# Loading and normalising x around the weight loads in a recurrent memory transformer block

## The chip, the cores and the metric

The kernel runs on one core of a Trainium2 chip. The core has a matrix engine (PE, with its own weight loads, PEld), a vector engine (DVE), a scalar engine (ACT), a general engine (POOL) and a queue engine (SP), and 16 DMA engines which all queues share. A DMA is issued from the queue of SP, ACT or POOL. The metric is the time of one execution on the device, in microseconds (us). The kernel before took 3471.91 us, the median of five runs from 3450.73 to 3481.48.

## The reference, cut to what matters

The reference computes a forward pass and all its gradients, in bf16. x has 2048 rows of 448 columns. Layer norm comes first, then an attention that walks over x in 64 segments of 32 rows and carries 8 memory rows from one segment to the next, then a gated feed-forward layer:

```python
for s in range(n_seg):                                   # 64 segments of 32 rows
    h = concatenate([mem, x[:, s*32:(s+1)*32]], axis=1)  # 8 memory rows and 32 of layernorm(x)
    q, k, v = h @ Wq, h @ Wk, h @ Wv                     # 448 -> 16 heads of 256
    p = softmax(where(mask, q @ k.T * scale, -1e9))
    o = (p @ v) @ Wo                                     # 16 * 256 -> 448
    mem = o[:, :8]                                       # goes into the next segment
    outs.append(o[:, 8:])
h  = x + attention(layernorm(x))
h2 = h + (silu(n @ w_gate) * (n @ w_up)) @ w_down        # n = layernorm(h)
```

The outputs are h2 and the gradients of x, mem0, the four attention weights and the three weights of the feed-forward layer. Segment s + 1 cannot start before segment s has given its memory rows, so the 64 segments are one chain, forwards and, for the gradients, backwards.

## The kernel before

The program has four phases: `forward_chain` (to about 1200 us of the trace), `ffn_phase`, `backward_chain` and `tail_phase`. Only the first is touched by the change. Everything lives in a few big arenas: `W` holds Wq, Wk, Wv and Wo (448 rows in `KC` = 4 chunks of 128, the last chunk half full and padded with zeros), `A` and `B` hold working tiles, and `A(kb, ...)` is a view that begins at that kilobyte. Two views at the same kilobytes are the same memory, and the framework makes the later user wait for the earlier.

How one segment runs (lines 375 to 476). The input of a segment stands in `hT_roll`, transposed: for each of the 4 chunks, 12 windows of 40 columns, 32 for rows of x and 8 for memory rows. `wpass` (line 353) multiplies Wq and then Wk with the segment's window: 128 matmuls each at line 360, cast out of PSUM by `k.evac` (line 75 on DVE, line 77 on ACT). Then come the scores (391), V (399), the softmax (403 to 416, with Exp on ACT at 409), the turned probabilities (420), the heads' outputs (428), and the output projection with Wo for the memory rows alone (437). The 8 memory rows are summed by a small matmul (446) and copied by DVE into the next window (449). Each segment stores qT, kT, the probabilities and V for the backward pass (451 to 454), and every fourth runs the projection for the 128 rows (462). `qT_b`, `kT_b` and `V_b` have two buffers each, used in turn. The heads' outputs of four segments stand in `xblk_b[t % 2]`, where t is the number of the group of 128 rows.

How x gets into the windows. `stats(t)` (line 311) loads tile t of x (128 rows) from SP or ACT in turn, into one of four places in `xblk_b[0]`; takes mean and variance on DVE (`ln_stats`, lines 82 and 84), the square root on ACT (86) and its reciprocal on DVE (87); writes the normalised tile into `xblk_b[1]` (319); and stores it to `XN` in DRAM (321). `prep_tile(t)` (line 338) reads it back with a DMA transpose on SP (342), and POOL copies it into four windows, one copy per chunk (345). The tile t + 2 is prepared in the first segment of group t (line 457), tiles 0 and 1 ahead of the loop.

What sets the order. The framework plans the order of every engine's instructions over the whole program, by priority and by its own estimate of when each can start, and then the order is fixed; an engine works through its list and stops at the first instruction that waits. What stands under `k.prio.crit()` has priority over the rest: in the kernel before, that is the chain of each segment. `tc.issue_after(ins)` makes the instructions under it stand behind `ins` in their engine's order. The weights are loaded from POOL, each as two DMAs (232, 233) followed by a memset of the padding (234), and Wo as one (328).

Of the kernel before, what the change touches and what calls it, by code (L numbers as in the profile page):

```python
# [229 lines left out]
def pad_rows(k, dst, src2d, eng):  # L230

    eng.dma_start(out=dst[:, 0:3, :], in_=src2d[0:3 * P, :].rearrange("(kc p) n -> p kc n", p=P))
    eng.dma_start(out=dst[0:64, 3, :], in_=src2d[3 * P:k.D, :])
    k.nc.gpsimd.memset(dst[64:P, 3, :], 0.0)
# [30 lines left out]
def forward_chain(k: _K):  # L265
    nc, tc = k.nc, k.tc
    S, D, M, H, Dh, HD = k.S, k.D, k.M, k.H, k.Dh, k.HD
    SEG, L, NSEG, NT, KC, DP, MC, DC = k.SEG, k.L, k.NSEG, k.NT, k.KC, k.DP, k.MC, k.DC
    X2 = k.aps["A_x"][0]
    MEM0 = k.aps["A_mem0"][0]  # L270
    ident, dr, sel, maskb = k.ident, k.dr, k.sel, k.maskb
    smal = k._small
# [8 lines left out]
    kT_b = [A(8 + 4 * i, 32, 64) for i in range(2)]  # L281
    V_b = [A(16 + 4 * i, 2048) for i in range(2)]
    stg_b = [A(24 + 4 * i, 2048) for i in range(2)]
    xblk_b = [A(32 + 8 * i, 32, P) for i in range(2)]
    mblk = A(48, 32, P)
    hT_flat = A(56, KC, NWIN * L + 24)
    hT_roll = hT_flat[:, :, 0:NWIN * L].rearrange("p k (w l) -> p k w l", l=L)
# [20 lines left out]
    nc.sync.dma_start(out=m0[0:M, 0:D], in_=MEM0)  # L308
    nc.vector.memset(m0[0:M, D:DP], 0.0)

    def stats(t):
        q = nc.sync if t % 2 == 0 else nc.scalar
        x_t = xblk_b[0].rearrange("p a b -> p (a b)")[:, (t % 4) * DP:(t % 4) * DP + D]
        q.dma_start(out=x_t, in_=X2[t * P:(t + 1) * P, :])
        mv = k.ln_stats(x_t, k.rstd1[:, t:t + 1], smal)
        xn = xblk_b[1].rearrange("p a b -> p (a b)")[:, (t % 4) * DP:(t % 4 + 1) * DP]
        if t < 4:
            nc.gpsimd.memset(xn[:, D:DP], 0.0)
        nc.vector.tensor_scalar(out=xn[:, 0:D], in0=x_t, scalar1=mv[:, 0:1], scalar2=k.rstd1[:, t:t + 1],
                                op0=ALU.subtract, op1=ALU.mult)  # L320
        q.dma_start(out=dr["XN"][t * P:(t + 1) * P, :], in_=xn)

    for t in range(2):
        stats(t)
    pad_rows(k, Wq_sb, k.Wq2, nc.gpsimd)
    pad_rows(k, Wk_sb, k.Wk2, nc.gpsimd)
    pad_rows(k, Wv_sb, k.Wv2, nc.gpsimd)
    nc.gpsimd.dma_start(out=Wo_sb, in_=k.Wo2.rearrange("(c p) d -> p c d", p=P))
    pm = k.ps1()
    pmh = pm[:].bitcast(BF16)  # L330
    for kc in range(KC):
        nc.tensor.transpose(pmh[:, kc * M:(kc + 1) * M], m0[0:M, kc * P:(kc + 1) * P], ident[0:M, 0:M])
    pm3 = pmh[:, 0:KC * M].rearrange("p (c m) -> p c m", m=M)
    nc.vector.tensor_copy(out=hT_roll[:, :, 0, SEG:L], in_=pm3)
    for t in range(2, NT):
        stats(t)

    def prep_tile(t):
        if t >= NT:
# [30 lines left out]
                                        in_=blk[:, 16 * hf:16 * hf + 16, :].rearrange("p c n -> p (c n)"))  # L370
            nc.gpsimd.dma_start(out=dr["X_o"][t][:, hf * 2048:(hf + 1) * 2048], in_=ot)

    prep_tile(0)
    prep_tile(1)
    for s in range(NSEG):
        t, r = divmod(s, 4)
        jm = s % 16
# [5 lines left out]
        with k.prio.crit():  # L383
# [57 lines left out]
            if s + 1 < NSEG:  # L441
                nc.vector.tensor_copy(out=om[:, 0:224], in_=pO[:, 0:224])
                nc.scalar.copy(out=om[:, 224:D], in_=pO[:, 224:D])
                pm = k.ps1()
                for kc in range(KC):
                    nc.tensor.matmul(pm[:, kc * M:(kc + 1) * M], lhsT=om[:, kc * P:(kc + 1) * P], rhs=sel[:, 0:M],  # L446
                                     start=True, stop=True)
                pm3 = pm[:, 0:KC * M].rearrange("p (c m) -> p c m", m=M)
                nc.vector.tensor_copy(out=hT_roll[:, :, (s + 1) % NWIN, SEG:L], in_=pm3)

        nc.gpsimd.dma_start(out=dr["QT"][s], in_=qT.rearrange("p c n -> p (c n)"))
        nc.sync.dma_start(out=dr["KT"][s], in_=kT.rearrange("p c n -> p (c n)"))
# [589 lines left out]
```

## Time and profile before

| what | value |
|---|---|
| median of five runs | 3471.91 us (3450.73 to 3481.48) |
| the profiled execution | 3470.52 us, its span 3468.7 us |
| granted PE clock, mean | 0.958 of full speed |
| PE busy, share of the span | 88% |
| DVE, ACT, POOL | 38%, 28%, 18% |
| first matmul of segment 0 | 39.19 us from the start |
| first matmul of segment 1 | 80.97 us |

Idle time of an engine is put down to what ended it: in `[35.80 <-POOL arA L345]` the engine was idle for 35.80 us, and what let it go was POOL's instruction of line 345 that wrote a tile of arena A. `SPq`, `ACTq` and `POOLq` are the queues that issue DMAs. The chain of work is followed back from the last instruction of the program, at each step to what released it, so what stands on it set the time. "issue" on it is time in which nothing that the profile shows was waited for. In the tables by stretch of time the columns are: the stretch, its length, busy time and number of instructions of PE, PEld, DVE, ACT and POOL, the granted PE clock, the busy share of the DMA engines, and GB/s.

### The profile page before, as it was taken

The numbers are of one execution on the slowest core, as the hardware profiler recorded it, in microseconds if no ns is written. First come the engines' busy times: TensorE is split into PE (matmuls) and PEld (weight loads), VectorE is DVE, ScalarE is ACT, GpSimd is POOL, SyncE is SP. The second block draws the span as 40 slices with busy tenths as digits, with TensorE's granted clock in tenths as the row PEclk, the third lists the DMA queues.
The fourth block names the chain that finished last, engine by engine and source line by source line (L and its number), as shares of the span: only waits on it lengthen the run. The fifth ranks groups of instructions, "written<-read, shape, count | busy, mean of one in ns | idle before, by whom it ended". The sixth has DMA issues, their size and how long they took to land.

```text
span 3468.7 us, 120965 instructions
## 1 busy us (share of the span) xinstructions
PE 3051.2 (88%) x55038; PEld 2061.0 (59%) x55038; DVE 1321.2 (38%) x2921; ACT 973.7 (28%) x2181; POOL 618.3 (18%) x1304
## 2 busy tenths in 40 slices
PE   3999999999999568992999998999999898998999
PEld 2677777777777445662666666666666454443444
DVE  4344444444444256771444444444444201111111
ACT  1333333333333222330333333333333102111100
POOL 3111111111111111111122122212211111111121
PEclk8999999999999879996999999999999899999999
DMA  7444633543444788899778777877877969788661
GB/s 263 131 130 130 177 127 130 161 145 129 153 134 142 162 187 178 195 219 232 147 155 176 156 172 164 174 155 169 169 166 154 301 195 195 166 177 171 160 247 38
DMA packets 997173, 583.91 MB, mean 168 GB/s; under 512 B 906100, under 2 KB 916420, under 8 KB 995060
## 3 DMA queue, kind: packets, MB, share of 16 engines
q1 hardware_dynamic: 926788, 340.27, 47.0%
q0 software_dynamic: 67568, 233.95, 19.9%
q8 instruction: 430, 7.05, 0.9%
q10 hardware_dynamic: 2304, 1.97, 0.2%
q14 instruction: 83, 0.68, 0.1%
HBM read 104.05 MB, written 250.19 MB: 102 GB/s over the span
## 4 chain that ended last, share of the span: by engine, by line
PE 61%; issue 13%; DMA 10%; DVE 8%; SPq 3%; ACT 2%; POOL 1%; ACTq 0%; DVEq 0%; POOLq 0%
PE psf L360 12%; PE po L756 8%; PE psf L399 6%; PE psf L713 5%; PE psf L691 4%; PE po L437 3%; PE fx L462 3%; PE fx L815 3%; PE psf L536 2%; PE psf L921 2%; PE psf L778 2%; PE psf L942 2%; PE psf L446 2%; DVE arA L75 2%; DVE arB L75 1%
## 5 line engine op out<-in xcount | busy, mean ns | idle before, releaser
L77 ACT CAST arA<-psf 128x320 bf16<-128x320 f32 (+4 forms) x1139 | 487.3, 447 | 1607.5 <-PE psf L360 423.5
L75 DVE CAST arA<-psf 128x384 bf16<-128x384 f32 (+6 forms) x1029 | 492.4, 496 | 1083.0 <-PE psf L921 363.7
L360 PE MATMUL psf<-arA,arW 128*128 128x40 bf16 x16384 | 433.4, 181 | 62.6 <-POOL arA L345 35.8
L360 PEld LDWEIGHTS <-arW 128*128 128x128 bf16 x16384 | 431.4, 97 | 77.5 <-issue 58.1
L756 PE MATMUL po<-arW,arA 128*32 128x448 bf16 x6144 | 359.7, 365 | 41.3 <-DVE arA L75 22.1
L921 PE MATMUL psf<-arW,arA 128*128 128x512 bf16 x990 | 254.1, 385 | 10.2 <-DMA arW<-X_k 4.6
L713 PE MATMUL psf<-arA,arW 128*128 128x40 bf16 x8192 | 218.7, 180 | 49.5 <-POOL arA L648 39.7
L399 PE MATMUL psf<-arW,arA 128*64 128x512 bf16 x2048 | 259.7, 382 | 0.0
L713 PEld LDWEIGHTS <-arW 128*128 128x128 bf16 x8192 | 214.4, 96 | 69.2 <-issue 68.7
L756 PEld LDWEIGHTS <-arA 128*32 128x32 bf16 x6144 | 156.0, 98 | 161.4 <-issue 32.7
L921 PEld LDWEIGHTS <-arA 128*128 128x128 bf16 x1440 | 136.1, 99 | 186.7 <-issue 42.5
L536 PE MATMUL psf<-arA,arW 128*128 128x256 bf16 x1344 | 164.1, 284 | 88.3 <-DMA arA<-arA 60.1
L536 PEld LDWEIGHTS <-arW 128*128 128x128 bf16 x1344 | 136.6, 102 | 118.1 <-issue 94.7
L399 PEld LDWEIGHTS <-arA 128*64 128x64 bf16 x2048 | 148.7, 111 | 65.2 <-issue 0.2
L75 DVE CAST arB<-psf 40x320 bf16<-40x320 f32 x320 | 107.8, 337 | 98.0 <-PE psf L428 64.5
L691 PEld LDWEIGHTS <-arW 128*128 128x128 bf16 x2048 | 88.6, 101 | 66.4 <-issue 62.8
L77 ACT CAST arB<-psf 128x96 bf16<-128x96 f32 (+1 forms) x320 | 98.2, 307 | 103.4 <-DVE arB L75 51.1
L723 ACT COPY arA<-psf 128x1024 bf16<-128x1024 bf16 x128 | 123.3, 1015 | 4.6 <-PE psf L722 3.0
L462 PE MATMUL fx<-arW,arA 128*128 128x448 bf16 x512 | 124.5, 353 | 0.0
L691 PE MATMUL psf<-arB,arW 128*128 128x80 bf16 x2048 | 99.5, 204 | 16.7 <-DVE arB L740 7.8
L437 PE MATMUL po<-arW,arB 128*8 128x448 bf16 x2048 | 109.4, 356 | 4.2 <-DVE arB L75 0.4
L942 PE MATMUL psf<-arW 128*128 128x448 bf16 x450 | 95.2, 361 | 5.7 <-DMA arW<-X_o 5.6
(232 smaller groups left out, 3769.0 us busy)
## 6 DMA issues: line engine op xcount, KB each, us to landing
QT<-arA POOLq DMA_DIRECT2D x64, 512.0 KB, 4.2
KT<-arA SPq DMA_DIRECT2D x64, 512.0 KB, 3.4
VG<-arA SPq DMA_DIRECT2D x64, 512.0 KB, 3.1
X_o<-arA POOLq DMA_DIRECT2D x40, 512.0 KB, 4.5
X_v<-arA POOLq DMA_DIRECT2D x32, 512.0 KB, 6.4
X_k<-arA POOLq DMA_DIRECT2D x32, 512.0 KB, 4.1
X_q<-arA POOLq DMA_DIRECT2D x32, 512.0 KB, 4.2
arW<-X_o SPq DMA_DIRECT2D x30, 512.0 KB, 14.2
```

What stands on the lines that cost most here:

```text
L75: nc.vector.tensor_copy(out=out, in_=in_)
L77: nc.scalar.copy(out=out, in_=in_)
L360: nc.tensor.matmul(pss[b][:, jj * L:(jj + 1) * L], lhsT=W_sb[:, kc, c * P:(c + 1) * P], rhs=hT_roll[:, kc, sl, :], start=(kc == 0), stop=( ...
L399: nc.tensor.matmul(pV[b][64 * g:64 * g + 64, 0:512], lhsT=hT_flat[:, kc, sl * L:sl * L + 64], rhs=Wv_sb[:, kc, n * 512:(n + 1) * 512], sta ...
L437: nc.tensor.matmul(pO[32 * (j % 4):32 * (j % 4) + M, 0:D], lhsT=o8[:, j, :], rhs=Wo_sb[:, cj(j), :], start=(j < 4), stop=(j >= MC - 4), sk ...
L462: nc.tensor.matmul(px[:, 0:D], lhsT=xblk[:, j, :], rhs=Wo_sb[:, cj(j), :], start=(j == 0), stop=(j == MC - 1))
L536: nc.tensor.matmul(ps[:, f2 * 256:(f2 + 1) * 256], lhsT=Wt[:, kc, c * P:(c + 1) * P], rhs=xT[:, kc, :], start=(kc == 0), stop=(kc == KC - 1))
L691: nc.tensor.matmul(ps[b][:, i * 2 * L:(i + 1) * 2 * L], lhsT=lhs[:, cl, :], rhs=rhs_bd[:, cl // 2, :, :].rearrange("p g n -> p (g n)"), st ...
L713: nc.tensor.matmul(pss[b][:, jj * L:(jj + 1) * L], lhsT=WoT_sb[:, kc, c * P:(c + 1) * P], rhs=do_roll[:, kc, sl, :], start=(kc == 0), stop ...
L756: nc.tensor.matmul(pH[32 * (j % 4):32 * (j % 4) + 32, 0:D], lhsT=blk[nm][:, j, r * SEG:(r + 1) * SEG], rhs=WT[:, cj(j), :], start=(nm == " ...
L921: nc.tensor.matmul(pa[2 * kc + g][:, 0:w], lhsT=lhs_of(b)[:, kc * P:(kc + 1) * P], rhs=rhs_of(b, g), start=(b == 0), stop=(b == nblk - 1), ...
L942: nc.tensor.matmul(pa[i][:, 0:D], lhsT=lhs_of(b, i), rhs=rhs_of(b), start=(bi == 0), stop=(bi == len(nblk) - 1))
```

## The change

The whole of x gets a place of its own, `xn_all`, 16 KB at `A(24)`, where it is loaded, normalised in place, and stored from. It lies over `stg_b` (first used in segment 3) and over `xblk_b[1]`, and the two halves of `xblk_b` are swapped, so that `xblk_b[1]` (now at `A(32)`) is first written in segment 4.

Tiles 0 and 1 are loaded by one DMA from SP, ahead of the weights. The weights are issued on POOL as before, but without the memsets in between; behind them, on the same queue, one DMA loads tiles 2 to 15; the three memsets come after that. The padding columns of all tiles are cleared by one memset on DVE.

The statistics of tiles 0 and 1 are taken under `k.prio.crit()`, with one square root for both, and the normalised tiles are turned by PE and copied into the windows by DVE and ACT (`by_pe`); they are still stored to XN, by one DMA for both. The statistics of tiles 2 to 15 are written behind segment 0's chain, and their `bn_stats` must stand behind the copy of line 449 (`to_h`) on DVE. They share one square root and one reciprocal, and are stored to XN by one DMA. Tile 2 is prepared in segment 2 instead of segment 0; the other tiles as before.

```diff
-    xblk_b = [A(32 + 8 * i, 32, P) for i in range(2)]
+    xblk_b = [A(40 - 8 * i, 32, P) for i in range(2)]
...
-    def stats(t):
-        q = nc.sync if t % 2 == 0 else nc.scalar
-        x_t = xblk_b[0].rearrange("p a b -> p (a b)")[:, (t % 4) * DP:(t % 4) * DP + D]
-        q.dma_start(out=x_t, in_=X2[t * P:(t + 1) * P, :])
-        mv = k.ln_stats(x_t, k.rstd1[:, t:t + 1], smal)
-        xn = xblk_b[1].rearrange("p a b -> p (a b)")[:, (t % 4) * DP:(t % 4 + 1) * DP]
...
-        q.dma_start(out=dr["XN"][t * P:(t + 1) * P, :], in_=xn)
-
-    for t in range(2):
-        stats(t)
-    pad_rows(k, Wq_sb, k.Wq2, nc.gpsimd)
-    pad_rows(k, Wk_sb, k.Wk2, nc.gpsimd)
-    pad_rows(k, Wv_sb, k.Wv2, nc.gpsimd)
+    xn_all = A(24, NT, DP)
+    x_rows = X2.rearrange("(t p) d -> p t d", p=P)
+    xn_rows = dr["XN"][0:S, :].rearrange("(t p) d -> p t d", p=P)
+    nc.sync.dma_start(out=xn_all[:, 0:2, 0:D], in_=x_rows[:, 0:2])
+    for Wd_sb, Ws in ((Wq_sb, k.Wq2), (Wk_sb, k.Wk2), (Wv_sb, k.Wv2)):
+        nc.gpsimd.dma_start(out=Wd_sb[:, 0:3, :], in_=Ws[0:3 * P, :].rearrange("(kc p) n -> p kc n", p=P))
+        nc.gpsimd.dma_start(out=Wd_sb[0:64, 3, :], in_=Ws[3 * P:D, :])
     nc.gpsimd.dma_start(out=Wo_sb, in_=k.Wo2.rearrange("(c p) d -> p c d", p=P))
...
-    for t in range(2, NT):
-        stats(t)
+    nc.gpsimd.dma_start(out=xn_all[:, 2:NT, 0:D], in_=x_rows[:, 2:NT])
+    nc.vector.memset(xn_all[:, :, D:DP], 0.0)
+    for Wd_sb in (Wq_sb, Wk_sb, Wv_sb):
+        nc.gpsimd.memset(Wd_sb[64:P, 3, :], 0.0)
+    mv_all = smal.tile([P, NT, nc.vector.BN_AGGR_DIM], FP32, name="mv_all", bufs=1)
+    sd_all = smal.tile([P, NT], FP32, name="sd_all", bufs=1)
+
+    def by_pe(t):
+        pt = k.ps1()[:].bitcast(BF16)
+        for kc in range(KC):
+            nc.tensor.transpose(pt[:, kc * P:(kc + 1) * P], xn_all[:, t, kc * P:(kc + 1) * P], ident[:, :])
+        for kc in range(KC):
+            k.evac(hT_roll[:, kc, 4 * t:4 * t + 4, 0:SEG], pt[:, kc * P:(kc + 1) * P].rearrange("p (g j) -> p g j", g=4),
+                   "vs"[kc % 2])
+
+    def stats(t0, t1, ins):
+
+        def placed(fn):
+            if ins is None:
+                return fn()
+            with tc.issue_after(ins):
+                return fn()
+        for t in range(t0, t1):
+            st6 = smal.tile([P, nc.vector.BN_STATS_DIM], FP32, name="stats")
+            placed(lambda: nc.vector.bn_stats(out=st6[:], in_=xn_all[:, t, 0:D]))
+            nc.vector.bn_aggr(out=mv_all[:, t, :], in_=st6[:])
+        nc.scalar.activation(out=sd_all[:, t0:t1], in_=mv_all[:, t0:t1, 1], func=ACT.Sqrt, bias=k.eps_t[:], scale=1.0)
+        nc.vector.reciprocal(out=k.rstd1[:, t0:t1], in_=sd_all[:, t0:t1])
+        for t in range(t0, t1):
+            nc.vector.tensor_scalar(out=xn_all[:, t, 0:D], in0=xn_all[:, t, 0:D], scalar1=mv_all[:, t, 0:1],
+                                    scalar2=k.rstd1[:, t:t + 1], op0=ALU.subtract, op1=ALU.mult)
+        nc.sync.dma_start(out=xn_rows[:, t0:t1], in_=xn_all[:, t0:t1])
+
+    with k.prio.crit():
+        stats(0, 2, None)
...
+        by_pe(0)
+        by_pe(1)
...
-    prep_tile(0)
-    prep_tile(1)
     for s in range(NSEG):
...
-                nc.vector.tensor_copy(out=hT_roll[:, :, (s + 1) % NWIN, SEG:L], in_=pm3)
-
+                to_h = nc.vector.tensor_copy(out=hT_roll[:, :, (s + 1) % NWIN, SEG:L], in_=pm3)
+        if s == 0:
+            stats(2, NT, to_h.ins)
...
-        if r == 0:
+        if (r == 0 and t > 0) or s == 2:
             prep_tile(t + 2)
```

The lines marked "..." under `stats(0, 2, None)` are those that turn mem0 by PE and copy it into window 0; they are the same as before and now stand under `k.prio.crit()`.

More of the change, by code (lines that the diff above doesn't have):

```diff
@@ L309, in forward_chain @@
     nc.vector.memset(m0[0:M, D:DP], 0.0)
-    def stats(t):
-        q = nc.sync if t % 2 == 0 else nc.scalar
-        x_t = xblk_b[0].rearrange("p a b -> p (a b)")[:, (t % 4) * DP:(t % 4) * DP + D]
-        q.dma_start(out=x_t, in_=X2[t * P:(t + 1) * P, :])
-        mv = k.ln_stats(x_t, k.rstd1[:, t:t + 1], smal)
-        xn = xblk_b[1].rearrange("p a b -> p (a b)")[:, (t % 4) * DP:(t % 4 + 1) * DP]
[L317 to L320, printed above, removed]
-        q.dma_start(out=dr["XN"][t * P:(t + 1) * P, :], in_=xn)
@@ L323, in forward_chain @@
-    for t in range(2):
-        stats(t)
-    pad_rows(k, Wq_sb, k.Wq2, nc.gpsimd)
-    pad_rows(k, Wk_sb, k.Wk2, nc.gpsimd)
-    pad_rows(k, Wv_sb, k.Wv2, nc.gpsimd)
-    nc.gpsimd.dma_start(out=Wo_sb, in_=k.Wo2.rearrange("(c p) d -> p c d", p=P))
[L329 to L334, printed above, removed]
@@ L338, in prep_tile @@
+    with k.prio.crit():
+        stats(0, 2, None)
+        pm = k.ps1()
+        pmh = pm[:].bitcast(BF16)
+        for kc in range(KC):
+            nc.tensor.transpose(pmh[:, kc * M:(kc + 1) * M], m0[0:M, kc * P:(kc + 1) * P], ident[0:M, 0:M])
+        pm3 = pmh[:, 0:KC * M].rearrange("p (c m) -> p c m", m=M)
+        nc.vector.tensor_copy(out=hT_roll[:, :, 0, SEG:L], in_=pm3)
+        by_pe(0)
+        by_pe(1)
     def prep_tile(t):
```

## The prediction

> **What bounds the kernel now.** I read the chain of work first, because the share page (PE busy 88% of the span) is an average over stages, and this change touches one stage only. The chain over the first 130 us (start, duration, what) is not PE there:
>
> ```profile
> 7.25 11.00 issue
> 18.64 10.66 DMA arA<-in_A_x_dram
> 31.50 20.56 DMA arA<-in_A_x_dram
> ...
> 55.63 3.28 DMA XN<-arA
> ...
> 60.29 3.02 DMA arA<-in_A_x_dram
> ...
> 77.22 1.72 PE po L437 x32
> ...
> 80.97 6.28 PE psf L360 x211
> ...
> 104.22 7.41 PE psf L360 x256
> ...
> 122.00 7.41 PE psf L360 x256
> ```
>
> Up to 60 us the chain is loads of x. 80.97 is the start of segment 1, 104.22 of segment 2, 122.00 of segment 3. The last copy of a memory result (L449) ends a chain of 63 at 1159.6; (1159.6 - 80.7)/62 = 17.40 us is a segment's usual time, so segment 0 (first matmul 39.19, end 80.97: 41.8 us) is 24 us too long, and nothing ran before 39.19. The timeline says why, engine by engine:
>
> ```profile
> 8.74 11.12 DVE L319 TENSOR_SCALAR arA<-arA,mv,rstd 128x448 bf16<-128x448 bf16 x3
> ...
> 14.51 3.53 POOL L234 MEMSET arW<- 64x4096 bf16 x1
> ...
> 39.19 7.28 PE L360 MATMUL psf<-arA,arW 128*128 128x40 bf16 x219 [35.80 <-POOL arA L345]
> ...
> 52.08 0.63 DVE L82 BATCH_NORM_STATS2 stats<-arA 128x6 f32<-128x448 bf16 x1 [18.16 <-DMA arA<-in_A_x_dram]
> ...
> 59.95 1.23 PE L360 MATMUL psf<-arA,arW 128*128 128x40 bf16 x32 [11.18 <-DVE arA L75]
> ```
>
> PE waits 35.8 us for POOL's copy of a turned tile; it then fills its PSUM banks and stops, because the casts that empty them (L75) stand on DVE behind a bn_stats that waits 18.16 us for a late x tile. What x waits for is the weights. Issues and time to landing, then the DMA share (the last two columns) by stretch:
>
> ```profile
> arW<-in_A_Wo_dram POOLq DMA_DIRECT2D x1, 3584.0 KB, 33.9
> arW<-in_A_Wq_dram POOLq DMA_DIRECT2D x1, 3072.0 KB, 11.0
> ...
> arW<-in_A_Wv_dram POOLq DMA_DIRECT2D x1, 512.0 KB, 24.6
> ```
>
> ```profile
> 0.00:5.00 5.00, 0.42 (x4) 0.25 (x4) 3.29 (x10) 0.00 (x0) 4.33 (x22) 1.00 0.34 93
> 5.00:52.00 47.00, 7.54 (x224) 7.18 (x225) 18.37 (x32) 3.21 (x9) 18.67 (x25) 0.99 1.00 350
> 52.00:81.00 29.00, 12.49 (x170) 8.48 (x170) 15.90 (x50) 10.10 (x22) 2.42 (x7) 0.66 0.48 150
> ```
>
> Wo is issued at 17.96 and lands at 51.9; the second part of Wv, issued at 13.97, at 38.6. From 5 to 52 us the DMA engines are full at 350 GB/s. So no order can bring segment 0 to its end much before Wo is in, about 52 us; the kernel ends it at 81. That 29 us is what the change can win; the rest of the run it leaves as it is.
>
> **The change, part by part.**
>
> *Start of segment 0.* Gone: for tiles 0 and 1 the way out to XN, back by a DMA transpose (L342) and through POOL (L345), which ends at 39. Added: 8 PE transposes (as L332's four, 0.42 us: about 1 us) and 8 evictions of 128x128, half on DVE, half on ACT (as L77's 128x96, 0.24 us: about 1 us on each). Tiles 0 and 1 come in one DMA behind mem0; the first x tiles landed at 3.78 in the trace, take 4.2. Two bn_stats and bn_aggr (1.15 + 0.3), the Sqrt table load 1.28, Sqrt 0.29, reciprocal 0.16: 7.5. The normalise then costs 0.38 each if free, but POOL is busy: the six weight issues (0.91 + 0.77 + 0.77 + 3 x 0.55 = 4.1) from about 3.3, Wo's 1.83, x's 14 tiles (between 0.55 and 1.83, take 0.9: nearest to half of Wo's descriptors), then three memsets of 3.53 in a row, to 20.7. In the rows, one normalise issued at 8.74 lasted 9.43 us and ended as the last memset did (18.04): so bounds 8.3 and 21.5 for the normalise, hT ready 11 to 24. Wq's second part lands near 16.8 as now. Segment 0 starts between 17 and 24; I take 23.
> [...]
>
> *Its end.* It does not matter which: from a segment's start to its output projection take 14.0 us (104.22 to 118.26): 37 if it starts at 23. Wv's landing comes in too: 38.6 at the latest (as now), plus 6.3 us from the first V matmul to the projection (111.97 to 118.26): 44.9. Both are before Wo. So everything above is hidden by Wo's load, with 4 us to spare; should that cover go, segment 1 moves by the excess.
> Wo's landing: moved by 52 us are 0.465 + 47 x 0.350 = 16.9 MB. In the changed order ahead of or beside Wo: weights 14.68, x tiles 0 and 1 0.23, their XN store 0.26, KT and VG of segment 0 0.52 each (SP's queue, same engines): 16.2 MB. 0.7 MB less is 1.9 us: 50.0; issues start 0.2 earlier: 49.8. Bounds: no KT or VG in front 47.0; as now 51.9. Then projection to segment 1's first matmul: 3.75 us warm (77.22 to 80.97), 5.2 at a granted clock of 0.5 (99.02 to 104.22). PE will have been idle for some 5 us; after the 11 us idle the rows show 0.50, so 5.2. Segment 1 starts at 55.0 (50.7 to 57.1): **gain 26.0** (23.9 to 30.2).
> [...]
>
> *Statistics of tiles 2 to 15, now behind to_h of segment 0.* x follows Wo in POOL's queue: 1.6 MB at 350 GB/s, 4.6 us: 54.4, just as to_h is written. The bn_stats stand behind to_h in DVE's order; if x is late, segment 1's first casts (1.4 us after its start) wait behind them. I take 1 us for it. The work: 14 x (0.51 + 0.08) + 14 x 0.38 + one Sqrt = 13.8 us of DVE, and two ACT table loads of 1.28. DVE is busy 14.2 of 36 us in segments 2 and 3, so there is room; lower bound 0, upper bound all in series, 16.4. The nearest row is the chain of the old segment 0 from 60 to 81, where statistics of eight tiles stood in it with 6.8 us, table loads included. The order is now written with the true gaps, but the tiles are nearly twice as many: 6. A cold start adds about 2 (old segment 1 had 23.25 - 17.40 = 5.9 over, 1.73 of it a stall in issue and 1.28 a table load; bounds 0 and 5.9). Segments 1 to 3: 3 x 17.40 + 6 + 1 + 2 = 61.2 against 139.96 - 80.97 = 59.0: **loss 2.2**.
>
> *The rest, with one answer.* SP and ACT lose 14 load issues and 14 stores of 0.35 to 0.4 us; one store of 1.8 MB on SP takes their place, waiting for the last normalise. Behind it on SP stand KT and VG stores; their buffers are used again two segments later, so up to a segment of delay costs nothing. prep_tile(2), moved from segment 0 to 2, passes on SP behind the KT and VG of two segments and on POOL its four copies (0.29 us) behind QT and P_all; it is due at segment 8, some 7 x 17.4 us after segment 1 begins, so its cover is over 80 us; if it were gone, PE would wait as at 39.19. The HC copies on POOL (81.01) wait for XN and come later; QT behind them is due two segments later, too. The pad memset on DVE (near L297's 0.38) falls before x lands. xblk's swapped halves: segments 0 to 3 no longer write where x is staged; no time of its own.
>
> **Sum**: 3470.5 (the profiled execution, 1.4 under the median of 3471.9; its span is 3468.7) - 26.0 + 2.2 = 3446.7: 3447.
>
> **Rivals.**
> A. *DVE waits for x.* One load of 14 tiles replaces many: nothing behind its semaphore starts until all of it is in. If it lands 10 us after to_h, the casts wait 9 us: 3456. For it: the same head-of-line wait is the 18.16 us row. Against: Wo is ahead of x in one queue, and landings kept issue order (Wq, Wk, Wv, Wo). It reaches no change at 7 us late.
> B. *The pad columns tie the first tiles to the late load.* If the program's dependences take the strided pad memset and the load of tiles 2 to 15 as overlapping, the transposes wait for 54.4: segment 0 from 57 to 75, gain 6, loss 2: 3466. Against: POOL's copies into windows 8 to 11 (L345 at 61.09) ran before L449's strided write at 80.72, which stands earlier in the program and spans those addresses without touching them.
> C. *A different order for the whole forward chain: slower.* The order on each engine is planned over the whole program; starting times change, so a non-critical operation may land ahead of a chain cast in each of the 60 later segments. One DVE operation costs 0.49 (L403) to 0.66 (a 480-column cast); 1 us per segment gives 3447 + 60 = 3507. It turns slower by 0.5% from (23.8 + 17.4)/60 = 0.69 us per segment. For it: segments already vary from 16.9 to 17.96. Against: none of the moved work recurs after segment 3.
> D. *Wo's cover is worse than thought*: the 1.6 MB of x share with it instead of queueing behind it, and it lands at 49.8 + 4.6 = 54.4: 3451, still faster. Against: the landings' order, as under A.
>
> **How the numbers follow.** The forecast with its own bounds (Wo 47.0 with a warm tail, no cost of statistics or clock: 3434; Wo 51.9, statistics in series, 5.9 of clock: 3462): 0.64. A 0.13, B 0.06, C 0.08, D 0.09. Five runs of the kernel lie from 3450.7 to 3481.5, so about 0.5% (17.4 us, 3454.5) is what a measurement tells from no change. Faster: 0.55 from the forecast, 0.06 from D, 0.05 from A: 0.66. Slower: C's 0.08. Same: 0.26. The range goes from 3430 (the best case and some scatter) to 3466 (A, D and the worst of the forecast; B's half and C left out).
>
> **What would show it.** Right: first L360 matmuls at 17 to 24, a PE wait for DMA of Wo before L437 that ends near 50, first matmul of segment 1 at 51 to 57, segments 1 to 3 together 58 to 65 us, later segments 17.4. The step on the normalise is wrong if it ends before 10; the step on Wo if it lands after 52; that on the statistics if DVE waits for x more than 2 us or segments 1 and 2 together exceed 45. The prediction falls if the spacing of L449 after segment 4 is not 17.4, or if PE's first matmul waits for x tiles 2 to 15.

## The result, and the profile after

The changed kernel takes 3465.45 us against 3473.85 us of the kernel before, both medians: a ratio of 0.9967, 95% interval 0.9954 to 0.9980. That is 11.5 us faster (7 to 16), where 3447 us and a gain of 24 us had been forecast. That the time lies just inside the upper end of the range (3430 to 3466) is luck: that end was drawn for A, D and the worst of the forecast, not for a loss behind segment 4. The profiled execution takes 3473.3 us (span 3471.5 us, granted clock 0.955); it is one of the slower ones, so the stages below say more than its total.

The chain of waits of the changed kernel (start, duration, what), from its start to segment 4:

```profile
7.31 45.33 DMA arW<-in_A_Wo_dram
52.68 3.12 PE po L460 x32
56.33 1.23 PE psf L469 x8
57.83 4.07 PE psf L385 x128
...
78.66 5.83 PE psf L385 x193
...
99.35 7.41 PE psf L385 x256
...
117.41 4.29 PE psf L385 x170
```

The loads of x are gone from it: one DMA, Wo's, now carries the chain from 7.31 to 52.64. Segment 1 starts at 57.83 (80.97 before), segment 4 at 117.41 (139.96 before). At segment 4 the changed kernel is 22.6 us ahead; 23.8 had been forecast. In all traces with the same start (those of experiments below among them) the copy that ends segment 3 comes at 116.3 to 118.6 with the change (five traces) and at 136.8 to 139.6 without (three): the lead is 20 us in the mean.

The timeline of the changed kernel, some lines of DVE, PE and POOL (start, duration, engine, line, operation; in brackets the idle time before and what ended it):

```profile
4.01 1.15 DVE L343 BATCH_NORM_STATS2 stats<-arA 128x6 f32<-128x448 bf16 x2 [1.52 <-DMA arA<-in_A_x_dram]
...
7.31 1.73 POOL L318 DMA_DIRECT2D arW<-in_A_Wo_dram  x1
...
7.80 1.63 DVE L348 TENSOR_SCALAR arA<-arA,mv_all,rstd 128x448 bf16<-128x448 bf16 x2
9.02 1.10 POOL L319 DMA_DIRECT2D arA<-in_A_x_dram  x1
...
9.19 1.03 PE L329 MATMUL psf<-ident,arA 128*128 128x128 bf16 x8 [3.03 <-DVE arA L348]
...
10.17 10.40 POOL L322 MEMSET arW<- 64x4096 bf16 x3
...
25.48 5.86 PE L385 MATMUL psf<-arA,arW 128*128 128x40 bf16 x200 [10.51 <-DMA arW<-in_A_Wk_dram]
...
30.59 0.56 POOL L475 DMA_DIRECT2D QT<-arA  x1 [9.50 <-issue]
...
52.68 3.09 PE L460 MATMUL po<-arW,arB 128*8 128x448 bf16 x32 [5.94 <-DMA arW<-in_A_Wo_dram]
...
57.69 1.14 DVE L343 BATCH_NORM_STATS2 stats<-arA 128x6 f32<-128x448 bf16 x2
```

Segment 0 now waits mostly for weights, longest for Wk (10.51 us) and Wo (5.94 us). The statistics of tiles 2 to 15 begin at 57.69, right behind the copy of the memory rows, without a wait for x. The stretches answer to those shown of before (the last two columns are the DMA share and GB/s):

```profile
4.00:52.50 48.50, 16.37 (x361) 12.16 (x362) 11.79 (x32) 8.76 (x18) 19.65 (x22) 0.89 1.00 350
52.50:57.80 5.30, 4.30 (x40) 2.03 (x40) 0.61 (x3) 0.34 (x1) 0.00 (x0) 0.71 0.81 276
```

350 GB/s for 48.5 us are 17.0 MB up to Wo's landing, where 16.2 MB had been counted; the records of single DMA packets give 17.3 MB from the start to 52.63.

So the start does what was forecast, within 1.2 us in this pair of traces, and about half of it is not there at the end. Behind segment 3 the order of instructions on every engine is the same in both kernels, but for nine pairs of neighbouring matmuls on PE which the trace puts within 0.03 us of each other, so the question was where the other half goes.

### The profile page after: what moved, and what is told of

Same layout as the page of the kernel before. It is cut to its first block, busy times and chain, and to the rows that moved or that the text cites. A ratio compares the mean times of both kernels' runs of the same rounds, so it can differ in the third digit from the quotient of the medians.

```text
span 3471.5 us, 120867 instructions
## 1 busy us (share of the span) xinstructions
PE 3054.1 (88%) x55046; PEld 2058.2 (59%) x55046; DVE 1308.7 (38%) x2912; ACT 971.1 (28%) x2171; POOL 616.1 (18%) x1293
## 3 DMA queue, kind: packets, MB, share of 16 engines
q1 hardware_dynamic: 925748, 340.37, 48.1%
q8 instruction: 430, 7.05, 0.9%
## 4 chain that ended last, share of the span: by engine, by line
PE 61%; issue 13%; DMA 10%; DVE 7%; SPq 4%; ACT 2%; POOL 2%; ACTq 0%; DVEq 0%; POOLq 0%
PE psf L385 12%; PE po L780 7%; PE psf L422 5%; PE psf L737 5%; PE psf L945 4%; PE psf L715 3%; PE po L460 3%; PE psf L560 3%; PE fx L486 3%; PE fx L839 3%; DVE arA L75 2%; PE psf L802 2%; SPq L910 2%; PE psf L469 2%; PE fx L626 2%
## 5 line engine op out<-in xcount | busy, mean ns | idle before, releaser
L560 PE MATMUL psf<-arA,arW 128*128 128x256 bf16 x1344 | 168.3, 288 | 93.4 <-DMA arA<-arA 57.3
L560 PEld LDWEIGHTS <-arW 128*128 128x128 bf16 x1344 | 138.4, 103 | 125.1 <-issue 95.1
L77 ACT CAST arB<-psf 128x96 bf16<-128x96 f32 (+1 forms) x320 | 98.2, 307 | 105.7 <-DVE arB L75 52.5
L715 PE MATMUL psf<-arB,arW 128*128 128x80 bf16 x2048 | 97.4, 201 | 18.2 <-DVE arB L764 8.7
## 6 DMA issues: line engine op xcount, KB each, us to landing
arW<-X_o SPq DMA_DIRECT2D x30, 512.0 KB, 12.2
```

What stands on the lines that cost most here:

```text
L77: nc.scalar.copy(out=out, in_=in_)
L560: nc.tensor.matmul(ps[:, f2 * 256:(f2 + 1) * 256], lhsT=Wt[:, kc, c * P:(c + 1) * P], rhs=xT[:, kc, :], start=(kc == 0), stop=(kc == KC - 1))
L715: nc.tensor.matmul(ps[b][:, i * 2 * L:(i + 1) * 2 * L], lhsT=lhs[:, cl, :], rhs=rhs_bd[:, cl // 2, :, :].rearrange("p g n -> p (g n)"), st ...
```

## The experiments

Times are ratios to the kernel before, run beside each on the same chip. "Old phase" says below that PE's instructions stand where they do in the kernel before, counted in blocks of 256. Both profiles have a DMA queue named for instructions (`q8 instruction: 430, 7.05, 0.9%`): 430 packets, each of 16 KB by the packet records. If it carries PE's 110,000 instructions, matmuls and weight loads, and nothing else, its 7.05 MB are 64 B for each, so 256 to a packet: an estimate from these numbers.

**16 more PE instructions in the kernel before.**

```diff
+    for _ in range(2):
+        pd = k.ps1()[:].bitcast(BF16)
+        for kc in range(KC):
+            nc.tensor.transpose(pd[:, kc * P:(kc + 1) * P], ident[:, :], ident[:, :])
     for t in range(2, NT):
         stats(t)
```

> The kernel before with eight PE transposes of the identity (16 PE instructions with their weight loads) added ahead of segment 0, their result not used: as many PE instructions as the change adds, in time in which PE is idle. If the missing half of the gain (22.6 us ahead at segment 4 in the traces, about 10 in the times) is lost because every later PE instruction stands 16 places further on in the instruction stream, this kernel is about 12 us slower than the kernel before (3474 to 3486). If the loss comes from somewhere else, it is within 4 us of the kernel before.

Measured: 1.0053 (1.0020 to 1.0085), 18 us slower, though the 16 instructions lie in a wait of 35.8 us. Where in the trace the 18 us lie was not settled. This pointed to the place in the stream, and is taken up again below.

**The change with tiles 0 and 1 turned by DMA, as before.** `by_pe(0)` and `by_pe(1)` are taken out, and `prep_tile(0)` and `prep_tile(1)` stand ahead of the loop again.

> The changed kernel with tiles 0 and 1 turned as before (store to XN, DMA transpose, POOL copies) instead of by PE. Theory of the prediction (segment 0's end is set by the landing of Wo, its start is covered): segment 0's first matmul moves from 14.5 to 30 to 36 us, its projection still starts at 52 to 54, segment 1 at 57 to 59, the time stays that of the changed kernel (3464) within 4 us. Rival (the start of segment 0 sets its end): segment 1 starts some 10 us later and the time is 3474. Theory that the 16 added PE instructions cost 12 us later: 3452.

Measured: 0.9979 (0.9950 to 1.0008). The memory rows of segment 0 are done at 62.91, 5.3 us later than in the changed kernel: turning the tiles by PE is worth 5 us there, Wo's load covers the rest. Segment 0 starts at 38.92, later than the 30 to 36 expected, and segment 1 at 63.2, 4 us beyond its range.

**The change without the statistics of tiles 2 to 15** (they are stored unnormalised, so this part of the computation is left out).

```diff
+    nc.vector.memset(k.rstd1[:, 2:NT], 1.0)
...
-            stats(2, NT, to_h.ins)
+            nc.sync.dma_start(out=xn_rows[:, 2:NT], in_=xn_all[:, 2:NT])
```

> The changed kernel without the statistics and the normalising of tiles 2 to 15 (x is stored to XN as it was loaded, the reciprocals are set to 1): what those cost under segments 1 and 2. In the prediction's sum they cost 6 us and the wait for x 1 us, so segment 4 should start 5 to 7 us earlier than in the changed kernel (117.4 to about 111.5) and the time be 3458. If they fit into gaps, nothing moves; if all of it stands on the chain, 14 to 16 us.

Measured: 0.9976 (0.9947 to 1.0005); segment 4 starts 2.6 us earlier than in the changed kernel, where 5 to 7 had been expected. But 1.5 of them are there at segment 1's start (56.31 against 57.83), before any of these statistics. Segments 1 to 3 take 58.3 us instead of 59.5, so the statistics cost them about 1 us.

**Wo in eight DMAs, in the order of use.**

```diff
-    nc.gpsimd.dma_start(out=Wo_sb, in_=k.Wo2.rearrange("(c p) d -> p c d", p=P))
+    wo_src = k.Wo2.rearrange("(c p) d -> p c d", p=P)
+    for i in range(4):
+        for g in range(2):
+            c0 = 16 * g + 4 * i
+            nc.gpsimd.dma_start(out=Wo_sb[:, c0:c0 + 4, :], in_=wo_src[:, c0:c0 + 4, :])
```

> The changed kernel with Wo loaded by eight DMAs in the order in which segment 0's projection uses it, instead of one. Theory that Wo's landing ends last in segment 0: the projection starts with the first quarter, some 8 us earlier (44 to 48 instead of 52.7), and ends within 1 us of the last quarter's landing, so segment 1 starts 2 to 4 us earlier than 57.8 (54 to 56), and the time is 2 to 4 us below the changed kernel's 3464 if that is kept. Rival that the projection is bound by something else: no change at segment 1.

Measured: 0.9997 (0.9968 to 1.0026). It fails for a reason of its own. POOL's timeline in this run:

```profile
7.32 1.54 POOL L322 DMA_DIRECT2D arW<-in_A_Wo_dram  x2
14.36 0.75 POOL L322 DMA_DIRECT2D arW<-in_A_Wo_dram  x1 [5.50 <-DMA arW<-in_A_Wq_dram]
...
39.59 10.41 POOL L326 MEMSET arW<- 64x4096 bf16 x3
```

In the trace's records POOL's DMAs signal their landing by eight semaphores in turn (105 to 112), so the ninth waits for the landing of the first, and so each one behind it: an order that the program makes, not the chip. The three memsets of padding, which stand behind them, come at 39.59 instead of 10.17, and PE waits 18.21 us for them. Segment 1 starts at 65.69. It says nothing on the question.

**A lag of 40 us, in both kernels.** Is a lead or a lag of the forward chain carried to the end, or does a stretch bound by the DMA engines swallow it?

```diff
-            for j in range(MC):
-                nc.tensor.matmul(pO[...], lhsT=o8[:, j, :], rhs=Wo_sb[:, cj(j), :], ...)
+            for rep in range(25 if s == 0 else 1):
+                for j in range(MC):
+                    nc.tensor.matmul(pO[...], lhsT=o8[:, j, :], rhs=Wo_sb[:, cj(j), :], ...)
```

> The changed kernel with the output projection of segment 0 done 25 times instead of once (the same result each time; 24 x 64 = 1536 more PE instructions, six whole instruction blocks of 16 KB). At 1.72 us for one repeat segment 1 starts about 41 us later, near 99, and everything behind it in the forward chain too. Theory 'absorbed': the stretch from the end of the forward chain to the start of the backward chain is bound by the DMA engines and takes up whatever lead or lag the forward chain has; then the backward chain starts where it does without the repeats (within 8 us) and the whole takes 3465 to 3480. Rival 'carried': the whole kernel is one chain, a lag of 41 us is paid in full, 3506, and the missing part of the gain is a cost of its own elsewhere. Half absorbed: 3485.

> The same 24 repeats of segment 0's output projection in the kernel before; segment 1 starts near 122 instead of 81. 'Absorbed': 3474 to 3490. 'Carried': 3515. Half absorbed: 3494. The two kernels should agree on the share that is carried, since it belongs to what stands behind the forward chain and not to the change.

Measured: 1.0074 (1.0045 to 1.0104) and 1.0092 (1.0060 to 1.0123). The copy of segment 3's memory rows comes 37.7 us later than in the changed kernel (154.7 against 117.0) and 32.8 us later than in the kernel before (172.4 against 139.6). The times rise by 37 us (0.0107 of 3474) and 32 us. Within some 10 us either way a lag is carried in full: "absorbed" falls for a lag, and the missing half of the gain is taken to be a cost of its own. That a lead passes, too, was not tested by itself; in the traces the stretch where it could be swallowed, from the end of the forward chain to the first feed-forward matmul, takes 74.5 us in the changed kernel and 77.1 in the kernel before.

**Whole blocks of PE instructions.** 128 unread transposes in the kernel before (as above, 32 rounds instead of 2), 120 in the changed one behind `by_pe(1)`; with the change's own 16 instructions both put PE back into the old phase.

> The kernel before with 128 unread PE transposes of the identity ahead of segment 0 (256 PE instructions, one whole block of 16 KB of PE's instruction stream, so that every later instruction stands in the same place of its block as in the kernel before). They lie under the 35.8 us that PE waits there anyway. Theory 'place in the instruction stream' (what the 16 added instructions cost before comes from where the block ends fall): as the kernel before, ratio 0.998 to 1.002, forward chain of 63 ends near 1159. Rival 'added instructions cost by themselves': as with 16 of them or more, 1.005 and up. Rival 'scatter': the 1.0053 with 16 was chance, 1.000 here as well and no difference between the phases of the three traces beyond 10 us.

> The changed kernel with 120 unread PE transposes of the identity behind the ones that turn tiles 0 and 1: with the 16 instructions that the change adds to PE, 256 in all, one whole block. About 12 us of PE, in the 10.5 us that PE waits for Wk and the 5.9 us that it waits for Wo. Theory 'place in the instruction stream': the segments go back to 17.4 each, the forward chain from segment 4 to its end takes 1020 us instead of 1026, and the kernel takes 3455 to 3460, ratio 0.994 to 0.996. Rival 'absorbed': whatever happens to the forward chain, the time stays at 3462 to 3467, ratio 0.997 to 0.998.

Measured: 1.0003 (0.9973 to 1.0034) and 0.9954 (0.9921 to 0.9987). A whole block costs nothing that could be measured where 16 instructions cost 18 us. In the changed kernel the gain is 16 us instead of 11.5, but the intervals overlap, and the forward chain from segment 4 takes 1022.5 us, not 1020.

What the traces have in common is sharper than the times. Seven times in the feed-forward stretch, at the start of a group of two tiles, PE stops for up to 10 us. The sixth stop, in PE's timeline of the changed kernel, and then of the one with 120 transposes:

```profile
1473.11 6.60 PE L560 MATMUL psf<-arA,arW 128*128 128x256 bf16 x59
1487.17 7.04 PE L560 MATMUL psf<-arA,arW 128*128 128x256 bf16 x39 [7.45 <-DVE arA L589]
```

```profile
1461.97 6.61 PE L564 MATMUL psf<-arA,arW 128*128 128x256 bf16 x59
1469.20 4.53 PE L564 MATMUL psf<-arA,arW 128*128 128x256 bf16 x40 [0.62 <-DVE arA L593]
```

Counted from the start of one matmul to the start of the next, this stop lasts 5.0 to 9.6 us in all nine traces with the store of DH on POOL whose PE stream stands 16 instructions further (the kernel before with 16 transposes among them), and at most 1.7 us in all eight in the old phase. What PE waits for stands in DVE's and POOL's timelines of the changed kernel:

```profile
1477.30 0.54 POOL L552 DMA_DIRECT2D DGP<-arA  x1 [5.34 <-DMA arA<-arW]
1477.83 0.54 POOL L631 DMA_DIRECT2D DH<-dh_t  x1
...
1485.83 0.69 DVE L262 SCALAR_TENSOR_TENSOR dh_t<-t1f,rstd,arW 128x448 f32<-128x448 f32 x1 [8.25 <-DMA DH<-dh_t]
1486.43 2.48 DVE L589 TENSOR_TENSOR arA<-psf,arW 128x512 bf16<-128x512 f32 x4
```

The store of DH stands on POOL behind a store that waits for a DMA transpose. `dh_t` has one buffer, so DVE's next write to it waits for that store to land, and behind it on DVE stand the products that empty PE's banks. The chain of waits through the feed-forward stretch of the changed kernel goes the same way, from a transpose over DH's store to PE, here at an earlier stop:

```profile
1298.41 6.45 DMA arA<-arW
1305.92 7.93 DMA DH<-dh_t
1315.29 6.95 PE psf L560 x48
```

**The change again, the old phase from the feed-forward stretch on, and padding on other engines.** The first is the changed kernel as it is. The second has the 240 PE instructions at the start of `ffn_phase`. The third adds 11 memsets of a 128x1 tile on POOL, the fourth the 120 transposes behind `by_pe(1)`, the 11 memsets, 9 small memsets on DVE and 26 small copies on ACT:

```diff
+    spare = smal.tile([P, 1], FP32, name="spare", bufs=1)
+    for _ in range(11):
+        nc.gpsimd.memset(spare[:], 0.0)
```

> The changed kernel once more, for a second trace of it and for times beside the next three on one chip. If the places found so far belong to the kernel and not to one execution, its trace shows them again: PE stops for 5 to 10 us about 255 us behind the first L560 matmul (an index-aligned gap of 0.6 to 0.9 in the kernels whose PE stream is in the old phase, 5.0 to 9.6 in the five whose PE stream stands 16 instructions later), segment 21 takes 19.5 to 20 us instead of 17.4, and the forward chain from segment 4 takes 1025 to 1027. Scatter would put these anywhere. Time 3462 to 3468.

> The 240 PE instructions not at the start but between the forward chain and the feed-forward stretch, where PE waits 52 us for a transpose of weights. Forward as in the changed kernel (1024 to 1027), the pause in the feed-forward stretch gone (the gap 0.6 to 0.9), the time 5 to 10 us under the changed kernel's, ratio 0.995 to 0.996. Rival: the pause belongs to what happened in the forward chain; it stays, ratio 0.997.

> The changed kernel with 11 memsets of an unread 128x1 tile on POOL at the start, so that POOL's later instructions stand in the same place of the stream as in the kernel before; PE is left as it is. Theory 'place of POOL's stream': P_all of segment 20, 2.6 to 3.0 us late in the changed kernels, is on time, segment 21 takes 17.4 to 17.9 instead of 19.7, the forward chain from segment 4 takes 1022 to 1024, and the pause of 5 to 10 us in the feed-forward stretch stays, because it is PE's. Time 2 to 4 us under the changed kernel's. Rival: the late P_all comes from something else, segment 21 stays at 19.7.

> All of it: 240 PE instructions behind the turned tiles (256 with the change's 16), 11 on POOL, 9 on DVE, 26 on ACT, so that on these four engines the stream behind the start stands as in the kernel before; SP has 15 fewer still. Theory 'place': forward chain from segment 4 to its end 1019 to 1022, no pause of 5 us or more in the feed-forward stretch, time 3474 - 22 = 3452, ratio 0.9935 to 0.9955: the lead of 22 us at segment 4 arrives at the end. Rival 'lost to DMA': ratio 0.9965 to 0.998 as the changed kernel.

Measured: 0.9951 (0.9926 to 0.9975), 0.9978 (0.9953 to 1.0003), 0.9836 (0.9797 to 0.9876) and 0.9971 (0.9953 to 0.9988). The changed kernel repeats itself: 1026.0 us for the forward chain from segment 4, 322.5 us from the first to the last L560 matmul, 5.0 us for the sixth stop. The 240 instructions ahead of the feed-forward stretch take the sixth stop away (0.2 us) and the time does not fall by anything that can be measured. And 11 memsets of 0.1 us make the kernel 57 us faster than the kernel before, where 2 to 4 us had been expected, while the same 11 memsets with other padding do nothing. No theory so far allows that.

One segment stands out in these traces: segment 20, counted from 0 (the expectations call it 21). With the 11 memsets and no other padding it takes 17.9 to 18.2 us (three traces, those of later experiments among them), where 17.4 to 17.9 had been expected. In the kernel before and its variants it takes 17.1 to 17.5, and in ten of the eleven other traces of the changed kernel and its variants 18.9 to 20.0. In these ten, PE stops in the middle of the segment for 1.6 to 1.9 us, and the profile shows nothing that it waits for:

```profile
400.66 2.52 PE L385 MATMUL psf<-arA,arW 128*128 128x40 bf16 x70 [1.82 <-issue]
```

**The pauses taken away.**

```diff
-            nc.gpsimd.dma_start(out=dr["DH"][rows, :], in_=dh_t[:])
+            nc.scalar.dma_start(out=dr["DH"][rows, :], in_=dh_t[:])
```

> The kernel before with the store of DH in the feed-forward stretch issued by ACT instead of POOL, so that it no longer stands behind a store that waits for a DMA transpose. Theory 'pauses': the seven pauses of PE (23 us in the kernel before) shrink to 10 or less, the time falls by 10 to 15 us, to 3455 to 3465. Rival 'the transposes bind there': the pauses stay within 4 us, or the time moves into the next groups, and the kernel takes 3470 to 3478.

> The same in the changed kernel, whose pauses were 33 to 36 us. Theory 'pauses': down to 10 or less as well, so that both kernels take the same time from the first L536 or L560 matmul to the last, and the changed one is ahead by the lead of the forward chain's end, about 16 us: 3440 to 3450, 20 to 25 less than without the edit. Rival 'lost elsewhere': it gains no more by the edit than the kernel before does, and the difference between the two stays 10 to 12.

> The changed kernel with 11 memsets on POOL once more. If the 3414 belongs to the kernel (where POOL's stream stands), it comes again, 3405 to 3425, with pauses under 18 us in the feed-forward stretch; if it was chance or one chip's, 3455 to 3465 with pauses near 33.

> Both edits. If the memsets help by shortening the pauses alone, nothing is left for them once the store is moved: the time is that of the changed kernel with the store on ACT, within 6 us. If they help in other stretches too (in their first trace the stretch behind L921 took 582 us instead of 589 to 606), 10 us or more under it, near 3405.

Measured: 0.9966 (0.9932 to 1.0001), 0.9891 (0.9857 to 0.9926), 0.9850 (0.9802 to 0.9899) and 0.9793 (0.9736 to 0.9850). How long DVE waits for DH (us in all, times), from the view of tile `dh_t` in the feed-forward stretch: the kernel before, the changed kernel, and the changed kernel with the store on ACT:

```profile
  DMA DH<-dh_t: 18.8, 6
```

```profile
  DMA DH<-dh_t: 36.3, 6
```

```profile
  DMA DH<-dh_t: 3.0, 1
```

In second traces of the first two (the kernel before with 256 PE instructions; the changed kernel again) it is 18.7 and 39.8. (These figures end with the last L536 or L560 matmul.) With the store on ACT the stretch takes 275.0 us in the kernel before and 280.4 us in the changed one, instead of 306 to 315 and 312 to 336, and the changed kernel is ahead by 0.0075 of the time: 26 us, with an interval of 17 to either side, since two ratios are compared (19 us by the medians). Its gain from the edit is 26 us, that of the kernel before 12 us; the times alone do not tell the difference of 14 (give or take 18) from nothing. The traces do show that the wait for DH is longer in the changed kernel (36.3 and 39.8 us against 18.8 and 18.7) and gone with the store on ACT. So it holds a part of what was given back; how large a part is not shown. The 3414 us with 11 memsets came again as 3412: it belongs to that kernel. With both edits the time is 43 us under the changed kernel with the store on ACT, so the memsets do not help by shortening these waits alone.

**Where the arenas lie.** The program's table of addresses had the answer to the 57 us. The change drops and adds small tiles, and the arenas behind them move: arW from 25120 to 25056. The 4 B tile of the 11 memsets moves it to 25088, the three small tiles of the full padding to 25152. Modulo 256 that is 32, 224, 0 and 64 (modulo 512: 32, 480, 0 and 64). Two edits move the arenas without touching an instruction:

```diff
-        sd = small.tile([P, 1], FP32, name="sd")
+        sd = small.tile([P, 1], FP32, name="sd", bufs=3)
```

```diff
-    sd_all = smal.tile([P, NT], FP32, name="sd_all", bufs=1)
+    sd_all = smal.tile([P, 2 * NT], FP32, name="sd_all", bufs=1)
```

> The kernel before with three buffers instead of four for the 4 B tile sd, so that every arena lies 32 B lower, arW at 25088 (0 modulo 512). No instruction differs. Theory 'place in SBUF': packets of 7168 B at 272 ns, feed-forward stretch from first to last L536 under 300 us instead of 306 to 315, and the kernel takes 3425 to 3440, ratio 0.986 to 0.990: what the 11 memsets gave the changed kernel. Rival 'place in the instruction stream': nothing moves, 3465 to 3475, ratio 0.998 to 1.002.

> The changed kernel with the tile sd_all twice as wide (64 B more, unread), so that the arenas lie where they do in the kernel before, arW at 25120 (32 modulo 512). No instruction differs from the changed kernel's. Theory 'place in SBUF': packets of 4096 B at 159 ns instead of 162, forward chain from segment 4 to its end 1018 to 1022 instead of 1026, feed-forward stretch 305 to 315 instead of 321, and the lead of 22 us of segment 4 arrives at the end: 3474 - 22 = 3452, ratio 0.992 to 0.995. Rival 'place in the instruction stream', which is the changed kernel's: 1026 and 321 as there, ratio 0.9965 to 0.998.

Measured: 0.9878 (0.9845 to 0.9911) and 0.9968 (0.9936 to 1.0001). The kernel before becomes 42 us faster (31 to 54) by one buffer less of a 4 B tile. The DMA queues of the kernel before, and then of the same with the arenas 32 B lower (packets, MB, share of 16 engines' span):

```profile
q1 hardware_dynamic: 926788, 340.27, 47.0%
q0 software_dynamic: 67568, 233.95, 19.9%
```

```profile
q1 hardware_dynamic: 926788, 340.27, 46.7%
q0 software_dynamic: 67568, 233.95, 19.5%
```

The packets are the same, in a span 36 us shorter, and take a smaller share of it. By the records of single packets, the median of those with 7168 B is 272 ns at base 0, 281 ns at 32 and at 64, 285 ns at 224. Base 0 has the shortest time; the rows do not tell 32 from 64, and what makes a packet take longer at another base is not shown. For the whole kernel, 0 instead of 32 is worth 42 us. Whether 256, 512 or another number is the multiple that counts was not tested.

But moving the changed kernel's arenas from 224 back to 32 gives it nothing: the forward chain still takes 1026.3 us, the feed-forward stretch 319.8 us, DVE waits 36.4 us for DH. So the base accounts for the 57 us within the intervals (42 us in the kernel before, and 11.5 us from the edit itself), and it does not explain the missing half of the gain: with both kernels at 32 the lead at the end is 11 us, with both at 0 it is 10 or 15, each give or take 11 to 20.

For the forward chain, base 0 does matter. In the three traces of the changed kernel with the 11 memsets, so with the arenas at 0, it takes 1018.1 to 1021.4 us from segment 4, no more than in the kernel before; with the same memsets and the arenas at 64 it takes 1026.5. Yet the kernel before is no faster there at 0 (1020.6) than at 32 (1020.0).

**The fastest version** is the changed kernel with the arenas at base 0 (by the tile of the 11 memsets) and the store of DH on ACT: 3386.7 us, 0.9793 (0.9736 to 0.9850), 72 us under the kernel before. It beats both kernels.

## Why the prediction was right and wrong

*Start of segment 0.* Right in outcome, wrong on the way. The normalise was expected to last about as long as POOL's memsets (up to 21.5, taken near the later bound); the two took 1.63 us and ended at 9.43, before the memsets began at 10.17; by the step's own sign (an end before 10) it was wrong. Of the two, the first took 1.33 us and ended at 9.13, just behind POOL's issue of Wo (9.04), the second 0.38. The tiles stand ready at 11, the first matmul runs at 14.49, when Wq has landed, and segment 0 then waits for Wk and Wo. Under Wo's load this costs nothing, as the step said; it had 4 us to spare, and PE's wait for Wo was 5.94.

*Wo's landing.* Wrong: 52.6 instead of 49.8, outside the bounds of 47.0 to 51.9. The bytes ahead of Wo were counted rightly; the step took x, which stands behind Wo in POOL's queue, to move only after it. By the packet records 1.0 MB of tiles 2 to 15 (220 of their 352 packets of 4480 B) had begun to move when Wo landed: 2.8 us at 350 GB/s. The store of QT, issued at 30.59 behind x, moved only from 54.4 on. Wo ends with sixteen packets of 896 B. They end between 48.1 and 52.1, in the mean at 48.8. That there is one of them on each of the 16 DMA engines, and that the engines which were done with Wo went on to x while the last still carried Wo, is an estimate from these numbers and times; the records do not name the engines.

*The tail to segment 1.* Right: 5.15 us (52.68 to 57.83) for 5.2. The granted clock was 0.50 from 52.6 to 55.0 and 0.71 in the mean of 52.5 to 57.8. With Wo late, segment 1 starts at 57.8 instead of 55.0, a gain of 23.1 instead of 26.0.

*Statistics under segments 1 to 3.* Right in sign, over-sized: these segments take 59.6 us, 61.2 had been expected, 59.0 before. The wait for x taken at 1 us is nil, and the statistics, taken at 6 us, cost these segments about 1. That the two errors cancel, 22.6 us of lead instead of 23.8, is luck; so in part is the 59.0, since the kernel before takes 55.8 and 56.4 in the other two traces with the same start.

*"The rest of the run it leaves as it is", with later segments at 17.4.* This is the step that failed. The mean of 59 later segments is 17.39 us in the changed kernel (1026.1 us in all) against 17.29 before (1020.0). The 17.39 looks like the 17.4 that was given as a sign of being right, but 17.40 was a mean which took in the slow segments 1 to 3 of the kernel before. No instruction is moved there, and still the chain takes 1022.5 to 1026.5 us in eleven traces of the changed kernel and its variants with the arenas elsewhere than at 0, and 1018.6 to 1022.4 in six of the kernel before and its variants: 5 us in the mean. The feed-forward stretch from its first to its last L536 or L560 matmul takes 312 to 336 us in ten of these traces against 306 to 315 in four (those with the store of DH on ACT or the arenas at 0 left out): 10 us. The other stretches differ by less than they scatter. These 15 us, give or take 6, are enough for the 9 to 11 that are missing. What was taken as the usual time of a stretch is not a property of its instructions alone.

*What causes it* is settled in part. One of the seven stops (at most 1.7 us against 5.0 to 9.6) goes with the place of PE's instructions. That the wait for DH carries the stops is shown; without it the lead at the end is 26 us, give or take 17, which is not clearly more than 11.5. That a lag is not swallowed, and that moving the arenas back by 64 B gives nothing, is shown, too. Open stays what lengthens the forward chain by 5 us, and the rest of DH's wait. Some 2 us of the 5 are in segment 20 alone, with its stop of PE, which the old phase of PE's stream does not remove. Putting back the instruction counts of PE, POOL, DVE and ACT (with the arenas at 64; SP's 15 fewer were not put back) left 1026.5 us. With the arenas at 0 the 5 us are gone, though the base by itself does nothing to the forward chain of the kernel before; why is not known.

*The rivals.* A and B did not occur: no wait for x on DVE, and PE turned the tiles at 9.19. D occurred in part: x shared with Wo, by 1.0 of its 1.6 MB, and Wo landed 2.8 us late instead of 4.6. The argument against it, that landings keep the order of issue, holds (x landed at 57.5, just as the statistics began) and does not exclude it. C comes nearest to what else went wrong, and its reason was wrong: the order behind segment 3 is unchanged, yet the forward chain is longer, by 0.1 us a segment in the mean, of which segment 20 alone makes some two fifths. A fifth case was missing altogether: the edit moves instructions and tiles that it does not touch.

## What to carry to other kernels

A lag at the start was carried to the end here, and a lead should be, though that was not tested by itself; but an edit also shifts every later instruction in its stream and every later tile in its memory; here this took or gave more than the edit itself (16 PE instructions cost 18 us, 32 B of memory 42 us, against 11.5). So, before judging an edit of 0.5%, compare the stages that it should not touch, and look at the bases of the big tiles: with the DMA engines busy for two thirds of the span (47.0 and 19.9% in two queues), arW at 25088 instead of 25120 (base 0 instead of 32) was worth 1.2%. A store behind a waiting store on the same queue, with one buffer, was a stop of the whole chain: it was worth 12 us (0 to 24) in the kernel before and 26 us (13 to 39) in the changed one to issue it elsewhere.

## What the runs showed of the hardware

- Moving all arenas of the kernel before by 32 B, with no other difference in the program, changed the time by 42 us (arW at 25088 instead of 25120: base 0 instead of 32, modulo 256). In the changed kernel base 224 instead of 32 made no difference that could be measured (0.9967 and 0.9968 of the kernel before).
- 16 unread PE instructions under a wait of 35.8 us made the kernel 18 us slower (7 to 29), 256 of them did not (1 us, from 9 faster to 12 slower).
- A load moved before the one in front of it on the same queue had landed: 1.0 MB of x, issued behind Wo, had begun to move when Wo landed at 52.63; x itself landed at 57.49.
- A normalise of 128x448, 0.38 us on DVE elsewhere, took 1.33 us beside POOL's issue of Wo and ended 0.09 us behind it; in the kernel before one took 9.43 us beside POOL's DMA issues and memsets and ended 0.13 us behind the last memset.
- In the feed-forward stretch the granted clock was 0.93 and 0.92 in two traces of the changed kernel, where PE idles for 41.9 and 42.5 us, 0.95 and 0.97 in two of the kernel before (34.5 and 35.5 us), 0.98 and 0.99 in these kernels with the store on ACT (12.2 and 9.0 us).
